# Attention and mixer in one kernel: the last two batches' round trip through DRAM without the turn before it, w2 copied to DRAM in an earlier batch, and another DMA rate in the first part of the plan

## The chip, the cores and the metric

The kernel runs on one core of one Trainium2 chip. The metric is the device time of one execution in microseconds. Before the change, three timed runs gave 572.02, 571.09 and 571.74 us (median 571.74). The profile is one more execution, with a time of 569.56 us of its own.

## The reference, cut to what matters

Four batches of 768 tokens. Attention has 8 heads of width 64; each token sees the tokens less than 16 away, and 24 block keys (the maximum over 32 keys each) with 24 block values (the mean over 32 values each). The mixer follows: a product over tokens, a residual, and a product over channels with a residual.

```python
k_sum = k.reshape(B, H, nb, block, D).max(axis=3)
v_sum = v.reshape(B, H, nb, block, D).mean(axis=3)
scores_l = np.where(mask_l, scale * q @ k.T, -1e9)
scores_s = scale * q @ k_sum.T + np.log(block)
a = softmax(concat(scores_l, scores_s))
x = (a @ concat(v, v_sum))            # (B, 768, 512)
h = np.maximum(x.T @ w_tok1, 0.0) @ w_tok2
u = x + h.T
out = u + np.maximum(u @ w_ch1, 0.0) @ w_ch2
```

All arrays are float32; the weights reach the kernel as pairs of 32-bit words of float64 numbers, so they are decoded on the chip.

## The kernel before, in words

**The plan.** Every piece of work is given to a list with an engine, a cost in microseconds, a rank, the tiles it reads and writes, and for a DMA its size in KB (`Plan.add`, L84). `Plan._order` (L119) then plays the list through once: each engine takes the ready work of lowest rank, and among equals the one listed first. A DMA occupies one shared stream at `RATE` = 250 KB per us and lands `LAND` = 2.2 us later (L72, L151). The order found is written out for each engine and is kept by it; what the chip then does earlier or later than planned does not change it. Tiles of one tag share a ring of buffers in listed order: a tile can be written once the last use of the tile so many places before it is over (`_link`, L107).

**Attention.** A step of `att_step` (L601) is "s" (scores), "e" (the exponentials are turned round so that the keys stand on partitions) or "a" (the weighted sum). `scores` (L401) takes a pair of heads and half of the tokens: 12 products of 64 queries by 120 columns (96 of the window, 24 blocks), then for each of six tiles `lowest` on VectorE (mask and minimum, L441) and `power` on ScalarE (exponential and sum, L451). For batches 0 and 1 the turn is done on TensorE (`turn`, L473). For batches 2 and 3 (`FAR` = 2) it is `turn_blocks` (L504): GpSimd has set the eight unused columns of each 128 to zero (L410), VectorE turns every block of 32 by 32 in place (L512), SyncE writes the tile to DRAM (`away`, L516, 393 KB), and four DMAs of a quarter of the partitions each bring it back with the blocks in their turned places (`fetch`, L525, L531), in runs of 32 numbers (128 bytes). `weighted` (L541) is 24 products on TensorE (L558) for each head and a scaling on VectorE (L571) into x.

**x.** For batches 2 and 3 x is turned on VectorE too (`turn_x`, L634), goes to DRAM in two parts (`xaway`, L645; 512 and 256 tokens for batch 2, 384 and 384 for batch 3), and `fetch_x` (L649) brings each part back in four DMAs in runs of 128 bytes. Batch 2 has it in tiles of tags `e` and `ot`, batch 3 directly in the tiles `u32` of tags `k` and `v`, where it stays to the end. `tok2` (L767) adds it to the product in PSUM on VectorE (L809), splits the sum into two parts (ScalarE L819, VectorE or GpSimd L825), and these feed `ch1`.

**The mixer.** For each half of a batch's tokens and each of 12 slices of the hidden width there is `ch1` (12 matmuls, L853), a relu on ScalarE and the remainder on VectorE (`h`, L865 and L870), and `ch2` (12 matmuls, L896). A half is 512 tokens (the wide half) or 256 (the narrow half). While batch b passes these 24 slots, attention and token mixing of batch b+1 run between the slots, held back so that a scores step does not start before the slot that it was listed in. `ch1` of the next slot is listed before `ch2` of this one. The last batch is done in another form (`last_sums` L1062, `last_mix` L1094): sums of its quarters on VectorE, products with sums of weight quarters, and w2 read back from copies in DRAM that `weight_away` (L1020) makes, 12 copies of 524 KB, in slots 12 to 23 of batch 2.

**The start.** TensorE runs 21 matmuls on zeros, the first keys, queries, the mask and values are loaded, and `w_tick` (L1379) loads and decodes the weights: ScalarE (L1426), VectorE or GpSimd (L1430) and three operations on VectorE (L1435, L1442, L1449). The listed sizes are 737 KB for keys, 393 for queries, 184 for the mask, 295 for values of one head, and 262 for one load of weights.

**Rings that matter here.** Tag `e` has three buffers, for the exponentials, their turned form, the turned x, and the fetched first part of x of batch 2. Scores and weighted sums share the PSUM banks `att`.

Of the kernel before, what the change touches and what calls it, by code (L numbers as in the profile page):

```python
# [69 lines left out]
class Plan:  # L70
    LATE = {"pe": 0.3, "act": 0.15, "dve": 0.15, "pool": 0.2, "sp": 0.0}
    RATE, LAND = 250.0, 2.2  # L72
# [46 lines left out]
    def _order(self):  # L119
# [19 lines left out]
        while events:  # L139
# [5 lines left out]
            for e, queue in queues.items():  # L145
# [45 lines left out]
def tile_attention_mixer(  # L191
# [28 lines left out]
    mask_sb = const.tile([P, 3, NC], F32, name="mask_sb")  # L220
# [51 lines left out]

    def load_q(p):
        b, hp = divmod(p, NP)
        q_t[p] = sbuf([P, S], "q", f"q_{p}", 2)
        return load(q_t[p], lambda t: t, q[b, hp], 393)

    def load_k(p):
        b, hp = divmod(p, NP)
        k_t[p] = sbuf([P, NT, NC], "k", f"k_{p}", 2)  # L280
        return load(k_t[p], lambda t: t, kw[b, hp], 737)
# [23 lines left out]
    def key_blocks(p):  # L305

        if p >= B * NP:
# [6 lines left out]
                in_=kt.t[:, :, 16 : 16 + QT].rearrange("p t (r c) -> p t r c", c=32),  # L314
# [7 lines left out]
                kt.t[:, :, WIN:], ks.t.unsqueeze(1).broadcast_to([P, NT, NB])  # L322
# [78 lines left out]
    def scores(p, g, behind=()):  # L401
# [4 lines left out]
        if p >= FAR * NP:  # L406
# [14 lines left out]
        def products():  # L421
            for i in range(TT // 2):
                for c in range(2):
                    t = 2 * (TT // 2 * g + i) + c
                    for j in range(2):
                        rows = slice(j * D, (j + 1) * D)
                        nc.tensor.matmul(  # L427
                            tiles[j].t[c * QT : (c + 1) * QT, i * NC : (i + 1) * NC],
                            lhsT=qt.t[rows, t * QT : (t + 1) * QT], rhs=kt.t[rows, t, :],
# [4 lines left out]
            "pe", 0.95, products, reads=[(qt, 0), (kt, 0), (kt, 1)],  # L434
            writes=[(t, 0) for t in tiles], rank=R_H, behind=behind,
        )

        def lowest(n, j, i):
# [3 lines left out]
                out=e.t[:, j, i * P : i * P + NC],  # L442
                in0=tiles[j].t[:, i * NC : (i + 1) * NC],
                in1=mask_sb[:, mv, :], op0=ALU.add, op1=ALU.min,
# [3 lines left out]
        def power(n, j, i):  # L448
            T = TT // 2 * g + i
            ei = e.t[:, j, i * P : i * P + NC]  # L450
# [22 lines left out]
    def turn(p, g):  # L473
# [3 lines left out]
        for j in range(2):  # L477
# [7 lines left out]
            eT_t[n, g] = view, [key]  # L485
# [18 lines left out]
    def turn_blocks(p, g):  # L504
# [4 lines left out]
        for j in range(2):  # L509
            eT_t[2 * p + j, g] = (lambda j=j: t_sb.t[:, j]), [(t_sb, r) for r in range(P // 32)]  # L510
        add(
            "dve", 1.05, lambda: nc.vector.transpose(flat(e.t), flat(e.t)),  # L512
            reads=[(e, "ends")], writes=[(e, part) for part in PARTS], rank=R_ATT,
        )
# [4 lines left out]

        fetch(away, t_sb, lambda: flat(t_sb.t), 150)  # L520
# [4 lines left out]
    def fetch(away, slot, view, kb, key=lambda r: r):  # L525


        def part(r):
            rows = slice(32 * r, 32 * (r + 1))
            src = away.t.rearrange("(q p) (t k) -> p t q k", p=32, k=P)  # L530
            nc.sync.dma_start(  # L531
                out=view()[rows].rearrange("p (t q c) -> p t q c", q=P // 32, c=32),
                in_=src[..., rows],
            )

        for r in range(P // 32):
            add(
                "sp", 0.4, lambda r=r: part(r), reads=[(away, 0)], writes=[(slot, key(r))], kb=kb,
            )

    def weighted(p):  # L541
        b, hp = divmod(p, NP)
        if hp % 2 == 0:
            x2_t[b, hp // 2] = sbuf([P, TT, 2, P], "x", f"x_{b}_{hp // 2}", 2)
        x2 = x2_t[b, hp // 2]
        x_t[b, hp] = x2, hp % 2
        for j in range(2):
# [4 lines left out]
            def products(n=n, pt=pt, v=v):  # L552
                pv = pt.t[:, : TT * D].rearrange("p (t d) -> p t d", d=D)
                for T in range(TT):
                    eT = eT_t[n, T // (TT // 2)][0]().rearrange("p (t c) -> p t c", c=P)
                    for c in range(2):
                        cs = slice(c * QT, (c + 1) * QT)
                        nc.tensor.matmul(  # L558
                            pv[cs, T], lhsT=eT[:NC, T % (TT // 2), cs],
# [10 lines left out]
            def scaled(rec=rec, pt=pt, j=j):  # L570
                nc.vector.tensor_tensor(  # L571
# [29 lines left out]
    def att_step(b, s, behind=()):  # L601
# [5 lines left out]
        elif kind == "a":  # L607
            weighted(p)
            if b >= FAR:
                turn_x(b, hp)  # L610
# [17 lines left out]
    def turn_x(b, p):  # L628

        x2, a = x_t[b, p]  # L630
        e = sbuf([P, S], "e", f"xb_{b}_{p}", 3)
        add(
            "dve", 1.05,
            lambda: nc.vector.transpose(  # L634
                e.t.rearrange("p (t c) -> p t c", c=P), x2.t[:, :, a, :]
            ),
# [1030 lines left out]
```

## Time and profile before

| | us |
|---|---|
| median of three runs | 571.74 |
| time of the profiled execution | 569.56 |
| its span in the trace | 567.6 |
| TensorE matmuls busy | 552.1 |
| VectorE busy | 355.6 |
| ScalarE busy | 258.2 |
| GpSimd busy | 258.9 |

The time of the profiled execution is 1.96 us longer than its span: that lies before the first and behind the last instruction. The granted TensorE clock is 1.0 throughout. By stages of the trace: to about 65 us the attention and token mixing of batch 0 with the first weights; 65 to 205 the channel mixing of batch 0 with the attention of batch 1 from about 126 on; 205 to 338 batch 1 with attention of batch 2; 338 to 475 batch 2 with attention of batch 3; 475 to the end the channel mixing of batch 3. The matmuls' ends are modelled, so that a busy share of 100% says only that the next matmul was at hand when the one before it ended. In rows of the timeline, the number in brackets is the idle time in front of an instruction and what ended it.

### The profile page before, as it was taken

To read this page: it belongs to the slowest core of one execution; us is meant where nothing else is said; L and a number is where in the kernel's file an instruction comes from. 1 tells how busy PE (TensorE), PEld (TensorE's weight loads), DVE (VectorE), ACT (ScalarE), POOL (GpSimd) and SP (SyncE) were. 2 spreads that over 40 slices of the span, in tenths; PEclk is the share of its full clock that TensorE was granted. 3 is DMA by queue.
4 is the path that set the end of the run, shared out by engine and by line. 5 is a ranking of instruction groups with operands and counts; after the bars stand their busy time and mean duration, and the time that the engine had idled before them with its cause. 6 is when DMAs were issued, how large, how long until landed. Compare 5 with 4: busy or idle time off the path is not lost.

```text
span 567.6 us, 12757 instructions
## 1 busy us (share of the span) xinstructions
PE 552.1 (97%) x4629; PEld 485.3 (85%) x4629; DVE 355.6 (63%) x982; ACT 258.2 (45%) x789; POOL 258.9 (46%) x325
## 2 busy tenths in 40 slices
PE   7789999999999999999999999999999999999997
PEld 4588888868989988777799997787789999999997
DVE  4698899997474246455563335445352484899984
ACT  4677675437385334232242314242233452567642
POOL 0236586753032510157797511048879711444111
PEclk9999999999999999999999999999999999999999
DMA  8953558653656017758795606677779663643621
GB/s 267 345 169 124 193 191 274 214 179 127 203 157 194 25 39 197 189 182 208 245 261 146 139 13 189 145 189 193 192 182 313 170 263 102 203 131 97 205 92 64
DMA packets 133774, 99.52 MB, mean 175 GB/s; under 512 B 88272, under 2 KB 112464, under 8 KB 133712
## 3 DMA queue, kind: packets, MB, share of 16 engines
q1 hardware_dynamic: 133568, 98.52, 58.2%
q8 instruction: 36, 0.59, 0.4%
q14 instruction: 26, 0.21, 0.1%
q10 hardware_dynamic: 144, 0.20, 0.1%
HBM read 68.60 MB, written 28.31 MB: 171 GB/s over the span
## 4 chain that ended last, share of the span: by engine, by line
PE 76%; DVE 11%; DMA 6%; ACT 3%; issue 2%; POOL 1%; SPq 1%; ACTq 0%; DVEq 0%
PE acc L896 21%; PE hp L853 20%; PE t1q L748 5%; PE up L792 4%; PE av L558 4%; PE pb L1126 3%; PE qb L1126 3%; PE sc L427 3%; DMA w<-in_w_ch 3%; PE qa L1126 2%; PE pc L1126 2%; PE pa L1126 2%; PE qc L1126 2%; DVE wb L1449 2%; ACT e L451 1%
## 5 line engine op out<-in xcount | busy, mean ns | idle before, releaser
L896 PE MATMUL acc<-h,w 128*128 128x512 f32 (+1 forms) x864 | 165.4, 341 | 1.4 <-DVE h L870 1.4
L853 PE MATMUL hp<-u,w 128*128 128x512 f32 (+1 forms) x864 | 163.6, 339 | 0.0
L896 PEld LDWEIGHTS acc<-h,w 128*128 128x128 f32 x864 | 133.4, 189 | 21.9 <-DVE h L870 1.8
L853 PEld LDWEIGHTS hp<-u,w 128*128 128x128 f32 x864 | 133.3, 188 | 20.2 <-issue 1.3
L451 ACT ACTIVATE e<-e,den 128x120 f32<-128x120 f32 x192 | 73.3, 385 | 55.1 <-DVE den L441 39.0
L870 DVE SCALAR_TENSOR_TENSOR h<-hp,h 128x512 fp32r<-128x512 f32 (+1 forms) x72 | 39.7, 552 | 83.8 <-ACT h L865 83.6
L865 ACT ACTIVATE h<-hp 128x512 fp32r<-128x512 f32 (+1 forms) x72 | 35.1, 488 | 114.4 <-PE hp L853 113.3
L973 POOL TENSOR_TENSOR s<-s,w 128x256 f32<-128x256 f32 x84 | 61.7, 741 | 5.0
L441 DVE CUSTOM_DVE_ANT_0 e<-sc,mask_sb 128x120 f32<-128x120 f32 x192 | 41.4, 277 | 13.0 <-PE sc L427 10.8
L1478 POOL TENSOR_TENSOR w<-wb,w 128x256 fp32r<-128x256 f32 x48 | 37.7, 805 | 19.0 <-ACT w L1472 18.8
L935 POOL TENSOR_TENSOR ot<-ot,u 128x512 f32<-128x512 f32 (+1 forms) x24 | 23.8, 1019 | 43.4 <-DVE ot L927 42.6
L792 PE MATMUL up<-wt,t 128*128 128x512 f32 (+2 forms) x192 | 39.0, 343 | 0.0
L451 ACT ACTIVATION_READ_ACCUMULATOR e<-e,den 128x1 f32 x192 | 36.2, 189 | 0.0
L734 POOL TENSOR_TENSOR xs<-x,xs 128x512 fp32r<-128x512 f32 x18 | 23.6, 1310 | 25.5 <-DMA v<-vs 17.9
L410 POOL MEMSET e<- 128x48 f32 x16 | 2.2, 138 | 67.8 <-DMA away<-e 32.7
L792 PEld LDWEIGHTS up<-wt,t 128*128 128x128 f32 x192 | 30.3, 189 | 2.6
L427 PE MATMUL sc<-k,q 64*64 64x120 f32 x768 | 28.1, 271 | 1.9 <-PE et L489 0.7
L427 PEld LDWEIGHTS sc<-k,q 64*64 64x64 f32 x768 | 20.5, 132 | 10.9 <-issue 7.0
L558 PEld LDWEIGHTS av<-v,eT 120*64 120x64 f32 x768 | 24.1, 138 | 6.7 <-issue 4.5
L558 PE MATMUL av<-v,eT 120*64 120x64 f32 x768 | 26.7, 224 | 2.7 <-issue 1.1
L1472 ACT ACTIVATE w<-wb 128x256 fp32r<-128x256 f32 x48 | 18.1, 413 | 23.0 <-DVE wb L1449 22.8
L748 PE MATMUL t1q<-xs,ws 128*128 128x256 f32 x216 | 28.5, 283 | 0.0
(128 smaller groups left out, 862.1 us busy)
## 6 DMA issues: line engine op xcount, KB each, us to landing
w<-in_w_ch SPq DMA_DIRECT2D x48, 256.0 KB
k<-in_kw SPq DMA_DIRECT2D x16, 720.0 KB
v<-in_vw SPq DMA_DIRECT2D x32, 288.0 KB
q<-in_q SPq DMA_DIRECT2D x16, 384.0 KB
away<-e SPq DMA_DIRECT2D x16, 384.0 KB
eT<-away SPq DMA_DIRECT2D x64, 96.0 KB
sums<-s SPq DMA_DIRECT2D x24, 256.0 KB
w2d<-w SPq DMA_DIRECT2D x12, 512.0 KB
```

What stands on the lines that cost most here:

```text
L427: nc.tensor.matmul(tiles[j].t[c * QT : (c + 1) * QT, i * NC : (i + 1) * NC], lhsT=qt.t[rows, t * QT : (t + 1) * QT], rhs=kt.t[rows, t, :], ...
L441: nc.vector.tensor_tensor_reduce(out=e.t[:, j, i * P : i * P + NC], in0=tiles[j].t[:, i * NC : (i + 1) * NC], in1=mask_sb[:, mv, :], op0=A ...
L451: nc.scalar.activation(ei, ei, AF.Exp, bias=den_t[n].t[:, 1, T : T + 1], scale=-1.0, accum_out=den_t[n].t[:, 0, T : T + 1],)
L558: nc.tensor.matmul(pv[cs, T], lhsT=eT[:NC, T % (TT // 2), cs], rhs=v.t[:NC, 2 * T + c], start=True, stop=True,)
L748: nc.tensor.matmul(pt.t[:, 2 * P * k : 2 * P * (k + 1)], lhsT=ws[:, wp, T, ks], rhs=xs[:, xp, T], start=(c == 0 and k == 0 and T == 0 and ...
L792: nc.tensor.matmul(pt.t[:, :nt], lhsT=t1.t[:, part, ks], rhs=wt2[w].t[:, k, h0 : h0 + nt], start=(far and k == 0 and i == 0), stop=(k == D ...
L853: nc.tensor.matmul(pt.t[:, :nt], lhsT=w1_t[f].t[:, w, c], rhs=us[c].t[:, part], start=(i == 0), stop=(i == len(ops) - 1),)
L870: lambda: nc.vector.scalar_tensor_tensor(out=h.t[:, 1], in0=pt.t[:, :nt], scalar=0.0, in1=h.t[:, 0].bitcast(F32), op0=ALU.max, op1=ALU.sub ...
L896: nc.tensor.matmul(slot.t[:, c0 : c0 + nt], lhsT=w2_t[f].t[:, w, o * P : (o + 1) * P], rhs=h.t[:, part], start=(f == 0 and w == 0 and part ...
L973: nc.gpsimd.tensor_tensor(out=out_, in0=left, in1=right, op=op)
L1126: nc.tensor.matmul(bank_.t[:, :HS], lhsT=w(i), rhs=x(j), start=first and n == 0, stop=True, skip_group_check=True,)
L1478: lambda hi=hi, lo=lo, source=source: nc.gpsimd.tensor_tensor(out=lo(), in0=source(), in1=hi().bitcast(F32), op=ALU.subtract),
```

## The change

1. `scores` for batches 2 and 3 multiplies by 128 columns instead of 120: the key tile gets eight more columns behind its last window, set to zero by GpSimd, and the mask tile has 128 columns of which the last eight are -1e30. The eight columns become zero by the exponential itself, and GpSimd's zeroing of the ends (L410) is gone. The exponentials are written in four blocks of 32 columns which stand apart in the tile.
2. `turn_blocks` writes the exponentials to DRAM as they are, `fetch` brings them back into the same tile in runs of 192 numbers (768 bytes), and VectorE then turns them into a second tile.
3. `turn_x` becomes `send_x`: x goes to DRAM unturned, straight from its tile, and `fetch_x` brings it back in runs of 256, 384 or 512 bytes. VectorE turns it afterwards: in place for batch 2, from a tile of tag `e` into `u32` for batch 3. The fetches of batch 3 are listed in slot 17, in the order in which the token mixing uses them, where before they were listed in slots 16 and 17.
4. The copies of w2 to DRAM are listed in slots 12 to 23 of batch 0 instead of batch 2.
5. The plan counts DMAs at 360 KB per us instead of 250 for those that it starts before 25 us of its own time.

```diff
-    RATE, LAND = 250.0, 2.2
+    RATE, FIRST, LAND = 250.0, 360.0, 2.2
-                    dma = max(dma, now) + w.kb / self.RATE
+                    dma = max(dma, now) + w.kb / (self.RATE if now > 25 else self.FIRST)
...
-            add(
-                "pool", 0.2,
-                lambda: nc.gpsimd.memset(
-                    e.t.rearrange("p j (t c) -> p (j t) c", c=P)[:, :, NC:], 0.0
-                ),
-                writes=[(e, "ends")], rank=R_LATER,
-            )
+        far = p >= FAR * NP
+        wide = P if far else NC
...
-                            tiles[j].t[c * QT : (c + 1) * QT, i * NC : (i + 1) * NC],
-                            lhsT=qt.t[rows, t * QT : (t + 1) * QT], rhs=kt.t[rows, t, :],
+                            tiles[j].t[c * QT : (c + 1) * QT, i * wide : (i + 1) * wide],
+                            lhsT=qt.t[rows, t * QT : (t + 1) * QT],
+                            rhs=kt.t[rows, t * NC : t * NC + wide],
...
-        add(
-            "dve", 1.05, lambda: nc.vector.transpose(flat(e.t), flat(e.t)),
-            reads=[(e, "ends")], writes=[(e, part) for part in PARTS], rank=R_ATT,
-        )
         add(
             "sp", 0.4, lambda: nc.sync.dma_start(out=away.t, in_=flat(e.t)),
             reads=[(e, part) for part in PARTS], writes=[(away, 0)], kb=393,
         )
-        fetch(away, t_sb, lambda: flat(t_sb.t), 150)
+        fetch(away, e, lambda: flat(e.t), 110)
+        add(
+            "dve", 1.05,
+            lambda: nc.vector.transpose(
+                flat(t_sb.t).rearrange("p (x a c) -> p a x c", a=P // 32, c=32),
+                flat(e.t).rearrange("p (a x c) -> p a x c", a=P // 32, c=32),
+            ),
+            reads=[(e, r) for r in range(P // 32)], writes=[(t_sb, 0)], rank=R_ATT,
+        )
...
-            src = away.t.rearrange("(q p) (t k) -> p t q k", p=32, k=P)
+            src = away.t.rearrange("(a p) (b c) -> p b a c", p=32, b=P // 32)
             nc.sync.dma_start(
-                out=view()[rows].rearrange("p (t q c) -> p t q c", q=P // 32, c=32),
-                in_=src[..., rows],
+                out=view()[rows].rearrange("p (a c) -> p a c", a=P // 32), in_=src[:, r]
             )
...
-        add(
-            "dve", 1.05,
-            lambda: nc.vector.transpose(
-                e.t.rearrange("p (t c) -> p t c", c=P), x2.t[:, :, a, :]
-            ),
-            reads=x_keys(b, p), writes=[(e, 0)], rank=R_ATT,
-        )
...
+        tag, bufs = (("e", 3), ("ot", 2))[half and not whole]
+        slot = sbuf([P, nt], tag, f"xT_{b}_{half}_{p}", bufs)
+        parts = [(slot, r) for r in range(P // 32)]
+        fetch(xa_t.pop((b, half, p)), slot, lambda: slot.t, nt // 6)
+        if whole:
+            to, j = u32[half, p // 2], p % 2
+            xT_t[b, half, p] = lambda: tokens(to.t[:, j]), [(to, j)]
+            add(
+                "dve", 0.07 + nt / 780,
+                lambda: nc.vector.transpose(tokens(to.t[:, j]), blocked(slot.t)),
+                reads=parts, writes=[(to, j)], rank=R_EVAC,
+            )
+        else:
+            xT_t[b, half, p] = lambda: blocked(slot.t), parts
+            add(
+                "dve", 0.07 + nt / 780, lambda: nc.vector.transpose(slot.t, slot.t),
+                writes=parts, rank=R_EVAC,
+            )
...
-            if b + 1 == B - 1 and slot in (16, 17):
-                for h in range(2):
-                    for p in (2 * slot - 32, 2 * slot - 31):
-                        fetch_x(b + 1, h, p)
+            if b + 1 == B - 1 and slot == 17:
+                for _, h, p in t2s:
+                    fetch_x(b + 1, h, p)
...
-            if b == B - 2 and slot >= NF:
+            if b == 0 and slot >= NF:
                 weight_away(slot - NF)
```

More of the change, by code (lines that the diff above doesn't have):

```diff
@@ L219, in tile_attention_mixer @@
     make_identity(nc, identf)
-    mask_sb = const.tile([P, 3, NC], F32, name="mask_sb")
+    mask_sb = const.tile([P, 3, P], F32, name="mask_sb")
+    nc.gpsimd.memset(mask_sb[:, :, NC:], -1.0e30)
     means = const.tile([WIN, 2 * NB - 2], F32, name="means")
@@ L271, in load, with windows @@
         )
+    def windows(t):
+        return t[:, : NT * NC].rearrange("p (t c) -> p t c", c=NC)
     def load_q(p):
@@ L279, in load_k @@
         b, hp = divmod(p, NP)
-        k_t[p] = sbuf([P, NT, NC], "k", f"k_{p}", 2)
-        return load(k_t[p], lambda t: t, kw[b, hp], 737)
+        slot = k_t[p] = sbuf([P, NT * NC + P - NC], "k", f"k_{p}", 2)
+        if b >= FAR:
+            add(
+                "pool", 0.1, lambda: nc.gpsimd.memset(slot.t[:, NT * NC :], 0.0),
+                writes=[(slot, "pad")], rank=R_ATT,
+            )
+        return load(slot, windows, kw[b, hp], 737)
     def load_v(n):
@@ L441, in lowest @@
             nc.vector.tensor_tensor_reduce(
-                out=e.t[:, j, i * P : i * P + NC],
-                in0=tiles[j].t[:, i * NC : (i + 1) * NC],
-                in1=mask_sb[:, mv, :], op0=ALU.add, op1=ALU.min,
+                out=block(j, i), in0=shaped(tiles[j].t[:, i * wide : (i + 1) * wide]),
+                in1=shaped(mask_sb[:, mv, :wide]), op0=ALU.add, op1=ALU.min,
                 scale=-1.0 / 8.0, scalar=3.0e38, accum_out=den_t[n].t[:, 1, T : T + 1],
@@ L537, in fetch @@
             add(
-                "sp", 0.4, lambda r=r: part(r), reads=[(away, 0)], writes=[(slot, key(r))], kb=kb,
+                "sp", 0.4, lambda r=r: part(r), reads=[(away, 0)], writes=[(slot, r)], kb=kb,
             )
@@ L647, in turn_x @@
             )
     def fetch_x(b, half, p):
-        if b == B - 1:
-            g, j = divmod(p, 2)
-            if not j:
-                u32[half, g] = sbuf([P, 2, HS], "kv"[g], f"u32_{half}_{g}", 2)
-            slot = u32[half, g]
-            xT_t[b, half, p] = lambda: slot.t[:, j], [(slot, (j, r)) for r in range(P // 32)]
-            fetch(
-                xa_t.pop((b, half, p)), slot, lambda: slot.t[:, j], HT[b][half] // 5,
-                lambda r: (j, r),
-            )
-            return
@@ L661, in fetch_x @@
-        tag, bufs = (("e", 3), ("ot", 2))[half]
-        slot = sbuf([P, HT[b][half]], tag, f"xT_{b}_{half}_{p}", bufs)
-        xT_t[b, half, p] = lambda: slot.t, [(slot, r) for r in range(P // 32)]
-        fetch(xa_t.pop((b, half, p)), slot, lambda: slot.t, HT[b][half] // 5)
+        nt, whole = HT[b][half], b == B - 1
+        if whole and (half, p // 2) not in u32:
+            u32[half, p // 2] = sbuf([P, 2, HS], "kv"[p // 2], f"u32_{half}_{p // 2}", 2)
+        tag, bufs = (("e", 3), ("ot", 2))[half and not whole]
@@ L809, in tok2 @@
                 lambda: nc.vector.tensor_tensor(
-                    out=xT(), in0=pt.t[:, :nt], in1=xT(), op=ALU.add
+                    out=xT(), in0=tokens(pt.t[:, :nt]), in1=xT(), op=ALU.add
                 ),
-                reads=[(pt, 0)], writes=parts + ([(u32[half, p // 2], p % 2)] if whole else []),
-                rank=R_EVAC,
+                reads=[(pt, 0)], writes=parts, rank=R_EVAC,
             )
@@ L824, in tok2 @@
                 eng, took,
-                lambda: between(eng, u.t[:, 1], xT(), u.t[:, 0].bitcast(F32), ALU.subtract),
+                lambda: (nc.vector, nc.gpsimd)[half].tensor_tensor(
+                    out=tokens(u.t[:, 1]), in0=xT(),
+                    in1=tokens(u.t[:, 0].bitcast(F32)), op=ALU.subtract,
+                ),
                 reads=[*parts, (u, 0)], writes=[(u, 1)], rank=R_EVAC,
```

83 lines of the change are left out of this document (60 added, 23 removed).

## The prediction

> **What bounds the kernel now.** I read the page first, then busy time by stage, then the chain of waits, then the timelines of the places that the change touches. In the page:
>
> ```profile
> span 567.6 us, 12757 instructions
> PE 552.1 (97%) x4629; PEld 485.3 (85%) x4629; DVE 355.6 (63%) x982; ACT 258.2 (45%) x789; POOL 258.9 (46%) x325
> DMA packets 133774, 99.52 MB, mean 175 GB/s; under 512 B 88272, under 2 KB 112464, under 8 KB 133712
> ```
>
> TensorE idles for 567.6 - 552.1 = 15.5 us in all, and nothing here makes its matmuls fewer. By stages (TensorE, weight loads, VectorE, ScalarE, GpSimd busy; clock, DMA share, GB/s):
>
> ```profile
> 0.00:20.00 20.00, 15.61 (x239) 9.94 (x241) 7.54 (x48) 10.67 (x45) 3.96 (x11) 1.00 0.92 295
> ...
> 80.00:100.00 20.00, 20.00 (x87) 16.14 (x86) 19.45 (x36) 12.58 (x29) 14.81 (x23) 1.00 0.81 252
> ...
> 140.00:160.00 20.00, 19.64 (x281) 18.00 (x279) 11.63 (x46) 9.41 (x38) 3.30 (x3) 1.00 0.55 179
> 160.00:180.00 20.00, 19.57 (x268) 18.73 (x269) 12.42 (x60) 13.36 (x52) 5.36 (x6) 1.00 0.65 202
> 180.00:200.00 20.00, 20.00 (x157) 19.29 (x156) 6.12 (x15) 8.05 (x17) 10.50 (x9) 1.00 0.17 49
> ...
> 380.00:400.00 20.00, 19.39 (x144) 15.34 (x143) 9.60 (x36) 6.56 (x27) 17.66 (x26) 1.00 0.73 185
> ```
>
> More than a quarter of it lies in the first 20 us (4.39), 0.79 in 140 to 180, and 0.61 at 380 to 400; of the stages from 205 to 475, in which batches 2 and 3 pass their attention, that last window is the only one short of 20.00. There TensorE is the bound, VectorE has 9.60 of 20 and the DMA engines are not full (0.73). So the part of the change that is longest in code can give back 0.61 us; the start, which only the plan's new rate touches, has more.
>
> **The change part by part.** *Runs through DRAM.* Runs of 128 bytes: 32 x 24 in each of 64 fetches of exponentials, 49,152, and 3,072 for each of 8 tiles of x, 24,576; together 73,728 of the 88,272 short packets. After it 64 x 32 x 4 = 8,192 runs of 768 bytes for the exponentials, 8,192 of 256 to 512 for x, and 8,192 more where x is written out. Who waits for them today:
>
> ```profile
> 373.43 6.17 DMA away<-e
> ...
> 379.61 0.58 SPq L531
> ...
> 381.64 3.91 DMA eT<-away
> 385.69 1.27 PE av L558 x36
> 341.54 0.78 PE sc L427 x24
> 456.79 4.17 PE up L792 x24
> 475.02 1.07 PE pa L1126 x6
> 148.16 6.51 DMA k<-in_kw
> ```
>
> ```profile
> 385.69 1.27 PE L558 MATMUL av<-v,eT 120*64 120x64 f32 x36 [0.61 <-DMA eT<-away]
> ```
>
> The fetch landed 3.91 us after the last of its four issues, and the later matmuls of one weighted sum waited 0.61 us for it, the only such wait among TensorE's. I take it away: **-0.6** (0 if it stays). [...]
>
> *Wider scores.* A pair of heads takes 0.78 us for half of the tokens. If columns set its pace, 128 instead of 120 add 0.78 x 8/120 = 0.052, 16 times: 0.83; if weight loads do, nothing. TensorE is the bound there, so **+0.8**, bounds 0 and 0.83. The same eight columns on ScalarE and VectorE (192 tiles of 385 and 277 ns, half of them far) add at most 96 x 26 and 96 x 18 ns, hidden under matmuls while VectorE stands at half. GpSimd loses 16 small fills and gains 8, at most 17.66 of 20 busy there.
>
> *The turns' new place.*
>
> ```profile
> L512 DVE STREAM_TRANSPOSE e<-e 128x768 f32<-128x768 f32 x16 | 15.6, 972 | 10.9 <-ACT e L451 9.5 <-POOL s L973 1.2
> L634 DVE STREAM_TRANSPOSE xb<-x 128x768 f32<-128x768 f32 x8 | 7.8, 978 | 0.3
> L451 ACT ACTIVATE e<-e,den 128x120 f32<-128x120 f32 x192 | 73.3, 385 | 55.1 <-DVE den L441 39.0 <-DMA v<-in_vw 16.0
> L441 DVE CUSTOM_DVE_ANT_0 e<-sc,mask_sb 128x120 f32<-128x120 f32 x192 | 41.4, 277 | 13.0 <-PE sc L427 10.8 <-DMA away<-e 2.1
> ```
>
> The blocks turned stay the same, 15.6 + 7.8 us; x's 8 turns become 16 shorter ones. But now each waits for a fetch, with VectorE's later work behind it in its order: the next `lowest`, and the remainder `h` for which `ch2` waits. A late fetch costs TensorE only what exceeds the cover: the next slot's 12 matmuls run while `h` is made.
>
> ```profile
> 378.82 2.96 PE L853 MATMUL hp<-u,w 128*128 128x512 f32 x12
> 381.62 2.96 PE L896 MATMUL acc<-h,w 128*128 128x512 f32 x12
> 382.45 0.69 DVE L870 SCALAR_TENSOR_TENSOR h<-hp,h 128x512 fp32r<-128x512 f32 x1 [1.42 <-ACT h L865]
> 318.82 0.69 DVE L809 TENSOR_TENSOR xT<-up,xT 128x512 f32<-128x512 f32 x1 [5.83 <-DMA xT<-xaway]
> 321.41 0.41 DVE L870 SCALAR_TENSOR_TENSOR h<-hp,h 128x256 fp32r<-128x256 f32 x1
> 425.44 0.39 ACT L865 ACTIVATE h<-hp 128x256 fp32r<-128x256 f32 x1 [0.67 <-PE hp L853]
> ```
>
> In the wide half slots of matmuls start 381.62 - 378.82 = 2.80 apart, and relu (estimated at 0.5 from its 0.39 in the narrow half) and remainder (0.69) take 1.2: cover 1.6. In the narrow half 1.4, half of that, less 0.39 and 0.41: 0.6. VectorE already stood 5.83 us for a fetch at 318.82, and the windows there show TensorE without a pause, because the list had put other matmuls ahead. So I take **0**; bounds 0 and +3.2 (rival B). The held buffers: a tile of exponentials is now busy until its turn, some fetch (4 to 6 us) longer, and the next scores wait for it; pairs of heads follow each other every 25 us (the weighted sums at 385.69 and, two pairs later, at 436.66 below), and the chain scores, exponentials 4, away 6, fetch 6, turn 1, sum 2 is about 20, so it fits without spare.
>
> *x of batch 3 at the end of batch 2.* Today its fetches run from 394 on; then they share `e`'s three buffers and cannot start before the last weighted sum:
>
> ```profile
> 436.66 1.62 PE L558 MATMUL av<-v,eT 120*64 120x64 f32 x48
> 394.20 2.96 SPq L531 DMA_DIRECT2D u<-xaway  x4
> 446.71 4.89 SPq L531 DMA_DIRECT2D u<-xaway  x7
> 462.11 0.55 DVE L809 TENSOR_TENSOR u<-up,u 128x384 f32<-128x384 f32 x1
> 468.00 1.02 DVE L975 SCALAR_TENSOR_TENSOR t<-t,t 128x384 fp32r<-128x384 f32 x2
> ```
>
> 32 issues at about 0.65 us (4.89 / 7 is 0.70, with other work of the queue between) are 21 us: from 437 to 458, landed and turned by 461. The last addition is at 462.11 now, so nothing is late by itself. Eight turns of about 0.49 us (384 of 768) delay VectorE's sums from 469 to perhaps 473; the last batch starts at 475.02, behind 14 us of channel matmuls. **0**; without that cover each us late is one lost.
>
> *w2's copies.*
>
> ```profile
> 461.35 3.08 SPq L1023 DMA_DIRECT2D w2d<-w  x4
> 460.00:470.00 10.00, 10.00 (x85) 10.00 (x84) 9.14 (x21) 5.68 (x14) 1.02 (x1) 1.00 0.61 237
> ```
>
> 524 KB at 237 GB/s is 2.2 us each, or 1.35 at a full share (237 / 0.61). Where they leave (424 to 464) TensorE has no idle time to win. In batch 0's second half, 134 to 205, one comes every 6 us: the share rises by 0.23 to 0.37, from 0.55 and 0.65 to nearly full, on the queue that brings batch 1's keys. DMA waits of 3.05 (block values), 6.51 (the quoted keys) and 1.90 us are on the chain there, 11.46 in all, and TensorE lost 0.36 + 0.43 us: 7%. Each longer by 2.2 gives 6.6 x 7% = **+0.5**; bounds 0 and 6.6.
>
> *The rate of the first 25 us.* By the listed sizes 5,016 KB go up to and with the first load of weights: planned to land at 5,016 / 250 + 2.2 = 22.3 us, now at 5,016 / 360 + 2.2 = 16.1. At the measured 295 GB/s it is 17.0. What the list does with it today:
>
> ```profile
> 19.87 0.56 DVE L571 TENSOR_TENSOR x<-av,rec 128x384 f32<-128x384 f32 x1 [4.70 <-PE av L558]
> 23.66 0.43 DVE L1430 TENSOR_SCALAR wt<-wt 128x512 f32<-128x512 f32 x1 [0.48 <-ACT wt L1426]
> ...
> 25.31 0.69 DVE L1449 SCALAR_TENSOR_TENSOR wt<-w,wt 128x512 int32<-128x512 int32 x1
> 30.74 0.40 ACT L451 ACTIVATE e<-e,den 128x120 f32<-128x120 f32 x1 [3.33 <-DVE den L441]
> 117.94 2.60 PE L896 MATMUL acc<-h,w 128*128 128x512 f32 x10 [1.40 <-DVE h L870]
> ```
>
> VectorE stands 4.70 us up to 19.87, begins decoding at 23.66, and the decodes then hold up ScalarE's exponentials for 3.33 us. One decode, four operations, is 25.31 + 0.69 - 23.66 = 2.3 us and would fit between 17.0 and 19.87. From 80 to 100 VectorE is busy 19.45 of 20 us and TensorE waits for it at 117.94, so time won there reaches the matmuls. I take one decode, less a little for the order around it, **-2.2**; bounds -4.7 (the whole gap) and +0.9 (planned at 16.1, there at 17.0, and VectorE standing).
>
> Sum: -0.6 + 0.8 + 0 + 0 + 0.5 - 2.2 = **-1.5**. The profiled execution is 569.56 (span 567.6 and 1.96 around it) and would be 568.1. The median of the runs is 2.2 above it; I carry the difference over: 571.74 - 1.5 = **570.2**.
>
> **The rivals.** *A, nothing in the start:* the wait at 19.87 is for a matmul, not for weights, and the list may fill the gap with something that was no bound. Then -0.6 + 0.8 + 0.5 = +0.7: 572.4. For it: only ScalarE's 3.33 us show that decoding came at a bad time. *B, slower: VectorE's list stands for fetches.* Place: the turns in narrow halves, 4 of exponentials and 12 of x; it decides once a fetch is later than its turn's place by more than 0.6 us. Four issues and landing took 5.94 us (379.61 to 385.55, chain of waits) where the plan now gives 4 x 110 / 250 + 2.2 = 3.96. If half of the 16 are late by 1.0, (1.0 - 0.6) x 8 = 3.2: 573.4. Against it: 5.83 us of the same wait cost nothing at 318.82. [...] *C, slower: copies in front of keys*, none covered: 570.2 + 6.6 - 0.5 = 576.3; against it, the plan counts the copies and puts matmuls ahead. *D, the whole gap of the start won:* 570.2 - 2.5 = 567.7.
>
> **How the numbers follow.** The forecast gets 0.42, A 0.18, B 0.21, C 0.07, D 0.12. About 0.2% (1.1 us) is what a measurement of this kernel can tell from no change. The forecast's own range is 569.0 to 571.5, with 0.7 of it below 570.6: 0.30 faster; with D 0.42. Same: 0.12 of the forecast, 0.14 of A and 0.02 of B, 0.28. Slower: the rest of A and B, and C, 0.30. The range 567.2 to 574.6 leaves out C and the tails of B and D.
>
> **What would show it.** Right: VectorE's gap before the first x gone and the first decode near 17 us; the dense channel matmuls some 2 us earlier; scores of batches 2 and 3 at 0.83; short packets about 31,000 or fewer; no TensorE idle time on a fetch between 205 and 475. Wrong: TensorE waiting for `h` with VectorE standing before a turn (B), key loads over 8 us between 140 and 180 (C), the first decode still after 22 us (A), or idle time before 475 because x of batch 3 came late.

## The result, and the profile after

The changed kernel took 574.1 us (median of nine runs, 572.96 to 575.23) where the kernel before took 571.09 beside it: a ratio of 1.0054, 95% interval 1.0034 to 1.0073. In a later group of runs (e9 below) it took 572.96 against 571.61, 1.0026 (1.0002 to 1.0050). So it is slower by 1.4 to 3 us, where 1.5 us faster was forecast. The profiled execution took 574.1 us. Three lines of its page:

```profile
span 572.3 us, 12735 instructions
...
PE 556.1 (97%) x4629; PEld 489.4 (86%) x4629; DVE 361.1 (63%) x990; ACT 260.1 (45%) x789; POOL 257.5 (45%) x318
...
DMA packets 82830, 99.52 MB, mean 174 GB/s; under 512 B 27216, under 2 KB 62032, under 8 KB 82768
```

The short packets went from 88,272 to 27,216, as the change says. TensorE's idle time is 572.3 - 556.1 = 16.2 us, hardly more than the 15.5 before; its matmuls' busy time grew by 4.0 us, so lost time can hide in matmuls that take longer. Where it lies, by the start of four matmul groups (first channel matmul of batch 0, first wide slot of batches 1 and 2, first product of the last batch), each read from TensorE's timeline:

| us | batch 0 | batch 1 | batch 2 | last batch | lengths between |
|---|---|---|---|---|---|
| before | 65.53 | 205.10 | 338.57 | 474.86 | 139.57, 133.47, 136.29 |
| changed | 70.20 | 207.87 | 342.00 | 479.59 | 137.67, 134.13, 137.59 |

Four differences add up to the 4.7 us between the last two starts: the first channel matmul comes 4.67 later, batch 0's stage is 1.90 shorter, batch 1's 0.66 longer and batch 2's 1.30 longer. The two profiled executions are 4.5 us apart where the medians are 3.0 apart: the one of before ran at the full clock throughout (a mean of 1.000), which 8 of 133 executions do (last section).

**The start.** Four-microsecond windows of the changed kernel (the busy time of the five engines, then granted clock, DMA share, GB/s), and its waits of TensorE and VectorE:

```profile
8.00:12.00 4.00, 1.72 (x51) 1.36 (x50) 2.97 (x21) 1.78 (x9) 0.00 (x0) 1.00 1.04 305
12.00:16.00 4.00, 3.17 (x49) 2.96 (x49) 0.63 (x8) 2.05 (x12) 0.00 (x0) 0.56 1.02 303
16.00:20.00 4.00, 4.00 (x72) 3.36 (x72) 2.41 (x15) 3.08 (x13) 1.59 (x2) 0.59 1.04 388
```

```profile
PE vm L348 <- DMA v<-in_vw: 5.2, 4, 2.3
PE t1p L739 <- DVE wt L1501: 2.7, 1, 2.7
```

```profile
DVE ks L321 <- DMA k<-in_kw: 10.1, 3, 4.2
DVE x L599 <- PE av L577: 1.4, 1, 1.4
```

The same windows of the kernel before:

```profile
8.00:12.00 4.00, 2.45 (x50) 1.60 (x42) 3.41 (x25) 3.12 (x17) 0.00 (x0) 1.00 1.05 278
12.00:16.00 4.00, 3.48 (x78) 2.93 (x78) 2.09 (x20) 3.98 (x20) 0.00 (x0) 1.00 1.03 281
16.00:20.00 4.00, 2.87 (x86) 2.63 (x88) 0.13 (x1) 2.29 (x10) 3.19 (x4) 1.00 1.03 382
```

VectorE's gap of 4.70 us ahead of the first x has shrunk to 1.4, as forecast, but the decoding did not move into it: the first decode is at 24.23, later than the 23.66 of before. VectorE stands for keys instead:

```profile
16.81 0.95 DVE L321 TENSOR_REDUCE ks<-k 128x24 f32<-128x768 f32 x1 [4.18 <-DMA k<-in_kw]
...
24.23 0.43 DVE L1482 TENSOR_SCALAR wt<-wt 128x512 f32<-128x512 f32 x1 [0.41 <-ACT wt L1478]
```

These waits are 10.1 us in three places, where the kernel before had one:

```profile
DVE ks L312 <- DMA k<-in_kw: 3.3, 1, 3.3
```

So 6.8 us more of VectorE's time go to waiting for keys, and 5.2 us of TensorE's to waiting for values, in a list that expects data at 360 KB per us while the DMA engines move 305 and 303 GB/s from 8 to 16 us; another 2.7 us of TensorE's go to waiting for decoded weights. And the granted clock, 1.00 before, is 0.56 and 0.59 from 12 to 20 us: from 12 to 16 us 49 small matmuls hold TensorE for 3.17 us, where 78 took 3.48.

**The end of batch 2.** TensorE, VectorE and SyncE's queue in the changed kernel:

```profile
456.14 0.62 PE L842 MATMUL up<-wt,t 128*128 128x384 f32 x2
457.05 0.97 PE L842 MATMUL up<-wt,t 128*128 128x384 f32 x4 [0.29 <-DVE t L725]
457.86 1.59 PE L948 MATMUL acc<-h,w 128*128 128x256 f32 x12
459.29 3.29 PE L842 MATMUL up<-wt,t 128*128 128x384 f32 x18
463.01 1.31 PE L842 MATMUL up<-wt,t 128*128 128x384 f32 x6 [0.44 <-DVE u L859]
```

```profile
455.32 0.58 DVE L687 STREAM_TRANSPOSE u<-xT 128x384 f32<-128x384 f32 x1 [0.33 <-DMA xT<-xaway]
...
458.45 0.58 DVE L687 STREAM_TRANSPOSE u<-xT 128x384 f32<-128x384 f32 x1 [1.45 <-DMA xT<-xaway]
...
462.42 0.54 DVE L859 TENSOR_TENSOR u<-up,u 128x384 f32<-128x384 f32 x1
```

```profile
434.39 6.21 SPq L550 DMA_DIRECT2D xT<-xaway  x6
440.77 1.21 SPq L666 DMA_DIRECT2D xaway<-x  x2
442.02 12.22 SPq L550 DMA_DIRECT2D xT<-xaway  x23
454.34 0.38 SPq L1066 DMA_DIRECT2D sums<-s  x1
454.77 1.39 SPq L550 DMA_DIRECT2D xT<-xaway  x3
```

The 32 issues for x of batch 3 fill the queue from 434 to 456. VectorE's turns stand for them, its splits and additions stand behind the turns, and the token products `up` wait 0.29 and 0.44 us for those and start piecewise.

**What stayed quiet.** Scores, two groups in a row, before and after; the turns; and the windows in which w2 is now copied:

```profile
345.24 0.85 PE L427 MATMUL sc<-k,q 64*64 64x120 f32 x24
346.02 3.06 PE L896 MATMUL acc<-h,w 128*128 128x512 f32 x12
```

```profile
344.90 0.89 PE L429 MATMUL sc<-k,q 64*64 64x128 f32 x24
345.72 3.07 PE L905 MATMUL hp<-u,w 128*128 128x512 f32 x12
```

```profile
L534 DVE STREAM_TRANSPOSE eT<-e 128x768 f32<-128x768 f32 x16 | 15.6, 972 | 6.3 <-DMA e<-away 6.3
L687 DVE STREAM_TRANSPOSE u<-xT 128x384 f32<-128x384 f32 x8 | 4.6, 575 | 6.0 <-DMA xT<-xaway 6.0
```

```profile
140.00:160.00 20.00, 20.00 (x242) 18.53 (x241) 12.21 (x53) 9.75 (x38) 5.11 (x4) 1.00 0.76 251
160.00:180.00 20.00, 20.00 (x291) 18.96 (x290) 11.52 (x59) 14.37 (x59) 5.28 (x6) 1.00 0.83 266
...
380.00:400.00 20.00, 19.99 (x173) 15.86 (x172) 9.08 (x27) 5.87 (x22) 15.85 (x22) 1.00 0.59 180
```

A group of scores takes 345.72 - 344.90 = 0.82 us where it took 0.78. VectorE stands 6.3 us in front of the turns of exponentials and TensorE loses nothing by it. From 140 to 180 and from 380 to 400 TensorE is full.

### The profile page after: what moved, and what is told of

Read it like the earlier page. It is cut to its first block, busy times and chain, and to the rows that moved or that the text cites. A ratio compares the mean times of both kernels' runs of the same rounds, so it can differ in the third digit from the quotient of the medians.

```text
span 572.3 us, 12735 instructions
## 1 busy us (share of the span) xinstructions
PE 556.1 (97%) x4629; PEld 489.4 (86%) x4629; DVE 361.1 (63%) x990; ACT 260.1 (45%) x789; POOL 257.5 (45%) x318
## 2 busy tenths in 40 slices
DMA packets 82830, 99.52 MB, mean 174 GB/s; under 512 B 27216, under 2 KB 62032, under 8 KB 82768
## 4 chain that ended last, share of the span: by engine, by line
PE 79%; DVE 9%; DMA 5%; issue 2%; ACT 2%; SPq 2%; POOL 1%; DVEq 0%; ACTq 0%
PE acc L948 23%; PE hp L905 22%; PE av L577 4%; PE sc L429 4%; PE up L842 4%; PE t1q L798 4%; PE qb L1178 3%; PE pb L1178 3%; PE qa L1178 2%; PE pc L1178 2%; PE pa L1178 2%; PE qc L1178 2%; DVE wb L1494 2%; DVE wb L1501 2%; DMA v<-in_vw 2%
## 5 line engine op out<-in xcount | busy, mean ns | idle before, releaser
L463 ACT ACTIVATE e<-e,den 128x120 f32<-128x120 f32 (+1 forms) x192 | 74.0, 387 | 39.4 <-DVE den L454 39.1
L454 DVE CUSTOM_DVE_ANT_0 e<-sc,mask_sb 128x120 f32<-128x120 f32 (+1 forms) x192 | 42.6, 280 | 8.1 <-PE sc L429 7.7
L429 PE MATMUL sc<-k,q 64*64 64x120 f32 (+1 forms) x768 | 28.9, 282 | 0.8 <-DVE den L454 0.8
L321 DVE TENSOR_REDUCE ks<-k 128x24 f32<-128x768 f32 x16 | 15.2, 947 | 22.8 <-DMA k<-in_kw 22.8
```

What stands on the lines that cost most here:

```text
L429: nc.tensor.matmul(tiles[j].t[c * QT : (c + 1) * QT, i * wide : (i + 1) * wide], lhsT=qt.t[rows, t * QT : (t + 1) * QT], rhs=kt.t[rows, t ...
L454: nc.vector.tensor_tensor_reduce(out=block(j, i), in0=shaped(tiles[j].t[:, i * wide : (i + 1) * wide]), in1=shaped(mask_sb[:, mv, :wide]), ...
L463: nc.scalar.activation(ei, ei, AF.Exp, bias=den_t[n].t[:, 1, T : T + 1], scale=-1.0, accum_out=den_t[n].t[:, 0, T : T + 1],)
```

## The experiments

All ratios are to the kernel before, run on the same chip, with 95% intervals. The runs came in four groups, each with its own runs of the kernel before: e1 to e4 and e13 to e15 on one chip, e5 to e8 and e9 to e12 on another. A difference of two kernels is taken within a group unless the text says otherwise.

### e1 to e3: the parts alone

e1, only the rate, in the kernel before:

```diff
-    RATE, LAND = 250.0, 2.2
+    RATE, FIRST, LAND = 250.0, 360.0, 2.2
...
-                    dma = max(dma, now) + w.kb / self.RATE
+                    dma = max(dma, now) + w.kb / (self.RATE if now > 25 else self.FIRST)
```

> The kernel before with one change: the plan counts DMAs that it starts before 25 us at 360 KB per us instead of 250. Theory (the loss is made in the start, by a list that expects keys and values earlier than they land): the first matmul of the first channel product, at 65.53 us before and 70.20 after, is at 69.5 to 70.5 here, and the time is 2.5 to 4.5 us above the kernel before. Rivals (the turns that wait for fetches, or the copies of w2, make the loss): within 1 us of the kernel before.

e2, the changed kernel with the old rate:

```diff
-    RATE, FIRST, LAND = 250.0, 360.0, 2.2
+    RATE, FIRST, LAND = 250.0, 250.0, 2.2
```

> The changed kernel with the old rate of 250 KB per us in the whole plan. Theory: the first channel product is back at 65.5 us; what is left is wider scores 16 x 0.045 = +0.7, weighted sums split in two +0.3, waits of 0.7 before the last batch, less the 0.6 us wait on a fetch that is gone: 1.1 us above the kernel before (0 to 2). Rivals: as slow as the changed kernel, 2.5 to 4 us above the kernel before.

e3, only w2's copies, in the kernel before:

```diff
-            if b == B - 2 and slot >= NF:
+            if b == 0 and slot >= NF:
```

> The kernel before with the copies of w2 listed in batch 0 instead of batch 2. Theory: within 1 us of the kernel before, as the changed kernel shows no new wait of TensorE between 140 and 205 us. Rival (copies in front of key loads): 2 to 6 us slower, with idle time of TensorE between 140 and 180 us.

e1: 572.51 us, 1.0022 (1.0000 to 1.0045). e2: 572.86, 1.0024 (0.9999 to 1.0049). e3: 571.21, 0.9983 (0.9962 to 1.0003). The rate alone costs about 1.3 us (0 to 2.6), where 2.5 to 4.5 were expected, and the rest without it about as much; w2 sooner costs nothing and may win a little. The first channel matmul misses both expectations: 66.81 in e1, not near 70, and 68.32 in e2, not back at 65.5. In e2's profile the stage of batch 2 is 137.9 us long, in e1's 136.1: that loss belongs to the new path of x and exponentials.

### e4 and e5: is the start's loss the granted clock?

e3 has the first 25 us of the kernel before in the same order, and yet its profile shows another clock (busy time of TensorE, clock, DMA share, GB/s):

```profile
12.00:16.00 4.00, 3.44 (x56) 0.75 1.02 323
16.00:20.00 4.00, 4.00 (x58) 0.50 1.04 383
20.00:24.00 4.00, 4.00 (x103) 0.90 0.33 112
```

(0.25 + 0.50 + 0.10) x 4 = 3.4 us of clock lost, with the first channel matmul at 67.74 in place of 65.53. e4 and e5 put matmuls on zeros into TensorE's pauses; nothing reads them.

e4, the changed kernel:

```diff
+            if p == 0 and g == 1:
+                for _ in range(14):
+                    nc.tensor.matmul(pw.t, lhsT=warm.t[:, :P], rhs=warm.t, start=True, stop=True)
...
```

> The changed kernel, the same list on every engine, but with 14 more matmuls on zeros (some 3 us) on TensorE directly behind the first two scores, where it stood idle 2.28 and 0.82 us for values. It separates the waiting from the clock: the granted clock of the changed kernel is 0.56 from 12 to 16 us and 0.59 from 16 to 20. If the lower clock behind the idle time is a cause of its own, the clock is 1.0 in those windows and the first channel product comes 1 to 3 us sooner (67 to 69 us); if only the late loads count, it stays at 70.2 within 0.4 and the time does not move.

e5, the kernel before: three such matmuls behind the first scores, two behind each of the first two turns.

```diff
+            for _ in range(3 if fill else 0):
+                nc.tensor.matmul(pw.t, lhsT=warm.t[:, :P], rhs=warm.t, start=True, stop=True)
...
+                for _ in range(2 if fill else 0):
+                    nc.tensor.matmul(pw.t, lhsT=warm.t[:, :P], rhs=warm.t, start=True, stop=True)
...
```

> The kernel before, with seven matmuls on zeros added to TensorE's list in its pauses of the start (three behind the first scores, two behind each of the first two turns); the result is untouched. Clock theory (idle time of TensorE in the start lowers the granted clock, and that is what makes one execution of the same list longer than another): the granted clock of 8 to 24 us stays near 1.0, the first channel matmul starts near 65.5 (65.53 in the profile of before, 67.74 with the same list at a lowered clock), the median falls by 1 to 2 us (ratio 0.9965 to 0.998) and its spread gets narrower. Rival (the pauses matter only as waits): the seven matmuls, 7 x 0.23 = 1.6 us in pauses of 0.7, 0.4 and 0.5 us, change nothing or cost some tenths: ratio 1.000 to 1.001.

e4: 571.83 us, 0.9994 (0.9978 to 1.0011); its clock is 1.00 from 8 to 24 us (and lowered later, from 24 to 36) and its first channel matmul at 67.45, as the clock theory had it. e5: 571.37, 1.0017 (0.9994 to 1.0040): no gain, though its mean granted clock rose from the 0.9936 of the kernel before beside it to 0.9962. The theory that filled pauses shorten the kernel fell here; where the time went that the clock should have given is not shown.

### e6: x of batch 3 written in quarters

In the changed kernel with the old rate, each part of x of batch 3 goes out in four DMAs and comes back in one, in rows of 1,536 bytes: 8 issues behind the last weighted sum in place of 32. TensorE's order is that of e2.

```diff
...
-        fetch(xa_t.pop((b, half, p)), slot, lambda: slot.t, nt // 6)
+        away = xa_t.pop((b, half, p))
+        if whole:
+            add(
+                "sp", 0.4, lambda: nc.sync.dma_start(out=slot.t, in_=away.t),
+                reads=[(away, r) for r in range(P // 32)], writes=parts, kb=nt // 2,
+            )
+        else:
+            fetch(away, slot, lambda: slot.t, nt // 6)
```

> The changed kernel with the rate of before, in which x of batch 3 is written to DRAM in four pieces for each part and comes back in one DMA with rows of 1,536 bytes in place of four; TensorE's order is the same as in e2. Theory (the end of batch 2 loses its 1.3 to 1.6 us because 32 issues for x of batch 3, 17 us of the queue, can begin only behind the last weighted sum): the 8 issues are through some 10 us sooner, TensorE's waits of 0.3 + 0.3 us before the token products go, and these run in one piece (9.8 us busy back to 9.2); the stage of batch 2 is 136.0 to 136.5 long in place of 137.9, and the median falls by 1.3 to 1.6 us against e2 (ratio to before about 0.9998). Rival (VectorE's eight turns and its order, not the queue, hold the additions back): the stage stays at 137.5 or more and the ratio at 1.002.

572.3 us, 1.0007 (0.9976 to 1.0037). The stage is 478.35 - 341.76 = 136.59 long where e2's was 137.94: 1.35 us less, by the same order of matmuls, and TensorE waits for nothing there. The time alone would not have settled it.

### e7 and e8: a rate near the measured one; w2 with filler

e7 is the kernel before with another rate; the second line of e1's edit belongs to it too.

```diff
-    RATE, LAND = 250.0, 2.2
+    RATE, FIRST, LAND = 250.0, 300.0, 2.2
...
```

> The kernel before with a rate of 300 KB per us for the DMAs of the first 25 us, near the 295 GB/s measured in the first 20 us, in place of 360. If 360 does harm because it is above the real rate and puts work at times at which its data isn't there, 300 has waits of TensorE for values in the start of under 1 us together (4.1 us with 360) and a ratio to before of 0.996 to 1.000. If any other order of the start loses against the one of before, it is 1.001 to 1.003, as with 360 (1.0022).

e8 is e3 with the filler of e5.

> The kernel before with the copies of w2 in batch 0 (e3, ratio 0.9983) and the seven matmuls on zeros of e5 in the pauses of the start. If the two add up: 0.9983 times the ratio of e5, by the clock theory 0.995 to 0.9965, the fastest of all so far. If the filler does nothing, 0.998 to 0.999.

e7: 570.98 us, 0.9997 (0.9973 to 1.0020). e8: 570.63, 0.9985 (0.9959 to 1.0011), as e3 without the filler. Another order of the start does not have to lose, but the reason given for e7 missed: TensorE still waits 2.2 us for values in its start, where under 1 was expected.

### e9 to e12: the changed kernel again, and the filler once more

e9 is the changed kernel, e10 is e4 with e6's edit, e11 is e1 with e4's 14 matmuls, e12 is e11 with e3's edit.

> The changed kernel once more, beside the next three on one chip, as their yardstick: 3.0 us above the kernel before (ratio 1.0054, 1.0034 to 1.0073) if what was measured first holds on another chip; granted clock of 0.5 to 0.8 somewhere between 12 and 36 us if the pause of TensorE for the values (3.1 us at 9.5 to 12.9) always lowers it.

> The changed kernel with the 14 matmuls on zeros of e4 (they fill TensorE's pause for the first values; the result is untouched) and with x of batch 3 written in four pieces and read in one (e6). If the two losses, the start's and the one at the end of batch 2, are separate: e4 against the changed kernel is worth 2.3 us and e6 against e2 shortened the stage by 1.35, together 3.6 us under e9 and 0.3 to 0.9 us under the kernel before (ratio 0.9985 to 0.9995). If they hide each other: 1.000 or more.

> The kernel before with the rate of 360 (e1, ratio 1.0022) and the 14 matmuls on zeros behind the first two scores. Theory (the rate's list loses by TensorE standing still for the values, which lowers its clock afterwards; the list itself isn't worse): 2 to 2.5 us under e1, ratio 0.998 to 0.999, the clock at 1.0 up to 24 us. Rival (the list is worse because of its waits for data, and filling them gains nothing; what e4 won came from the chip that it ran on): 1.001 to 1.003.

> e11 with the copies of w2 in batch 0 as well (e3, ratio 0.9983). If what each brings adds up, 0.9965 to 0.9975, faster than the kernel before beyond the interval; if the copies bring nothing by themselves, as e11.

e9: 572.96 us, 1.0026, less than half of the 3.0 us of the first measurement; its clock is lowered in the same windows. e10: 571.25, 1.0001 (0.9981 to 1.0021), 1.7 below e9 where 3.6 were expected, and e6's edit explains 1.35 of it. e11: 572.81, 1.0029 (0.9999 to 1.0059), no better than e1, though its clock was 1.00 up to 24 us. e12: 570.48, 0.9991 (0.9970 to 1.0013), better than e11 and short of the sum. The filler earns nothing on the rate's list either; most of what e4 seemed to win against the 574.1 of the first measurement did not hold within one group.

### e13 to e15: the two losses mended

e13 is e3 with the rate of 300, e14 the changed kernel with 300, e15 is e14 with e6's edit.

> The kernel before with a rate of 300 for the first 25 us and the copies of w2 in batch 0. e3 (w2 alone) gave 0.9983 and e7 (300 alone) 0.9997. If the two add up: 0.998, about 570.5 us where the kernel before has 571.5; if w2's copies were chance: 1.000.

> The changed kernel with a rate of 300 in place of 360, all else as changed. Over 104 executions of the kernel before, the time rises by 0.32 us for each 0.001 that the mean granted clock falls (569.3 at 1.0); with 360 the mean clock is 0.9906 in the changed kernel and 0.9894 in e1, with 300 it was 0.9922 in e7, where the time was 0.3 under the kernel before. If the start's loss comes from the rate being above the real one: 1 to 1.5 us under the changed kernel, ratio 1.001 to 1.003, the stage of batch 2 still 137.6 to 137.9 long. Rival (any reordering of the start costs as much): as the changed kernel, 1.0026 to 1.0054.

> e14 with x of batch 3 written in four pieces and read in one, as in e6: the whole change with its two losses mended. The stage of batch 2 comes to 136.3 to 136.6 and the time to 1.2 to 1.4 us under e14: ratio 0.9985 to 1.0005. What is left against the kernel before is the wider scores, 16 x 0.045 = 0.7 us. Rival (the end of batch 2 was not the loss): no difference from e14.

e13: 569.02 us, 0.9962 (0.9943 to 0.9980), faster than both kernels. e14: 570.97, 0.9990 (0.9972 to 1.0008). e15: 569.61, 0.9971 (0.9954 to 0.9987). All three came out faster than expected. VectorE's waits in e13, with its first x and its first decoding operation; TensorE's waits for values in e13, and for values and decoded weights in e14; and the end of batch 2 in e15, with the queue:

```profile
DVE ks L312 <- DMA k<-in_kw: 3.1, 1, 3.1
...
DVE x L571 <- PE av L558: 0.5, 1, 0.5
```

```profile
18.06 0.91 DVE L312 TENSOR_REDUCE ks<-k 128x24 f32<-128x768 f32 x1
...
19.78 1.26 DVE L571 TENSOR_TENSOR x<-av,rec 128x384 f32<-128x384 f32 x2 [0.46 <-PE av L558]
...
21.48 0.43 DVE L1430 TENSOR_SCALAR wt<-wt 128x512 f32<-128x512 f32 x1
```

```profile
PE vm L339 <- DMA v<-in_vw: 4.2, 3, 3.2
```

```profile
PE vm L348 <- DMA v<-in_vw: 2.6, 3, 1.0
PE t1p L739 <- DVE wt L1501: 1.2, 1, 1.2
```

```profile
453.46 4.33 PE L866 MATMUL up<-wt,t 128*128 128x384 f32 x24
...
473.05 1.23 PE L1202 MATMUL pa<-u,w 128*128 128x384 f32 x6
```

```profile
433.10 2.42 SPq L701 DMA_DIRECT2D xT<-xaway  x3
435.67 3.67 SPq L667 DMA_DIRECT2D xaway<-x  x8
439.44 5.21 SPq L701 DMA_DIRECT2D xT<-xaway  x5
```

At 300 the gap in front of x shrinks too (0.5 us in e13, 1.4 in e14, no more than 0.8 in e15) and no wait for keys stands in its place (3.0 to 3.1 us in all three, 3.3 before). What moves ahead of x is not the decoding but the minima and key sums of the next heads, and decoding, behind x as before, begins at 21.48 in e13 where it began at 23.66. TensorE still waits for values. In e15 the fetches are issued by 445 and the products run 24 in a row. In all three the clock is lowered in the start as well (e13: 0.60 from 12 to 16 us), so the lower clock does not make a list lose by itself.

The profiles of all runs, read up to batch 0's last slot, show two effects apart. "Clock" is the time lost to a lowered clock in the first 64 us; "idle" is TensorE's idle time before the first channel matmul and within batch 0's stage (from there to the first wide slot of batch 1):

| | rate | w2 copied in batch | clock, us | first channel matmul | idle | stage of batch 0 | idle |
|---|---|---|---|---|---|---|---|
| before | 250 | 2 | 0 | 65.53 | 9.0 | 139.57 | 2.2 |
| e3 | 250 | 0 | 3.4 | 67.74 | 7.5 | 140.08 | 2.7 |
| e7 | 300 | 2 | 5.1 | 66.40 | 6.6 | 140.33 | 3.0 |
| e1 | 360 | 2 | 3.4 | 66.81 | 8.7 | 139.80 | 2.7 |
| e13 | 300 | 0 | 3.4 | 65.58 | 7.4 | 137.89 | 1.0 |
| e14 | 300 | 0 | 5.1 | 66.88 | 7.1 | 137.74 | 0.9 |
| changed | 360 | 0 | 5.1 | 70.20 | 10.9 | 137.67 | 0.8 |

First, the rate: e14 and the changed kernel lose the same clock, and the changed kernel comes 3.3 us later (e9, again with 5.1, 3.6 later), with 3.8 us more idle time; so in these executions it is the waits and not the clock that separate 360 from 300. In the kernel before, TensorE's idle time there is 2.1 us more at 360 (e1) than at 300 (e7). Secondly, batch 0's stage is 137.6 to 138.3 us long in all eight profiles with a higher rate and w2's copies in batch 0, and 139.4 to 140.8 in the nine with one of them or neither. The two together win some 2 us there that neither wins alone.

The parts add up within the last group: e13 is 2.50 us below the kernel before; the wider scores add 0.7, which gives -1.8, and e15 measured -1.91; x of batch 3 late adds e14 - e15 = 1.36, which gives -0.55. Each of these times is known to about 1 us, so that the agreement to 0.1 is in part luck. From there to the changed kernel there is only the rate, 300 to 360: 1.9 us by e9's distance from its own kernel before (1.35 + 0.55), 3.6 by the first measurement's (3.01 + 0.55), each across groups. Against the old rate of 250 (e2, 1.0024) 360 costs the changed kernel only 0.1 to 1.7 us: in the profiles, both with 5.1 us of clock lost, it reaches the first channel matmul 1.9 us later than e2 (70.20, 68.32) and has a stage of batch 0 that is 1.7 us shorter (137.67, 139.40).

## Why the prediction was wrong

**Right.** The fetch stall (-0.6): the window 380 to 400 is full (19.99 of 20). That the fetch would land sooner was the author's assumption, which no run of before shows; in the changed kernel, where a turn waits for four issues in a row, issues and landing take 3.9 to 4.8 us (311.20 to 315.17, 386.41 to 391.23, 429.36 to 433.22), where the prediction read 5.94. The wider scores (+0.8): 0.82 - 0.78 is 0.04 to 0.05 a group, 0.7 in 16. The turns' new place (0): 6.3 us of VectorE standing before the turns of exponentials reached no matmul, for the profile shows no wait of TensorE from 205 to 440. Short packets: 27,216 against "31,000 or fewer".

**The rate of the first 25 us (-2.2) failed,** in two steps. The first is the step that put a decode into VectorE's gap ("would fit between 17.0 and 19.87"). Nowhere in the changed kernel, e1, e13 and e14 does the decoding begin before the first x: it is at 24.23, 21.62, 21.48 and 23.44. Its first operation on VectorE also stands behind one on ScalarE, which begins at 22.97 before and at 23.53 in the changed kernel and which the prediction left out. The list may fill the gap with other work, as rival A said. The second is the step that took 360 for nearly harmless: the bound "+0.9 (planned at 16.1, there at 17.0, and VectorE standing)" priced one late load, the weights. But a list made for 360 also expects keys and values, which come before the weights, too soon, and an order that is kept stands for them: 6.8 us more of VectorE's time for keys than before, and on TensorE 5.2 us for values and 2.7 for decoded weights, where e14, at 300, has 2.6 and 1.2. The prediction had the number that says so, 295 GB/s beside 360, and used it for one load only. Measured: about +1.3 alone (e1, 0 to 2.6) where -2.2 stood; e14 against the changed kernel puts 360 at 1.9 to 3.6 us above 300.

That e13 wins 2.5 us, near the 2.2 of the forecast, does not bear out the sum. The rate of 300 alone (e7) won nothing that could be measured, and a good part of e13's gain is the stage of batch 0 (1.7 us shorter in its profile), which needs w2's copies as well, a term that stood at +0.5. The wait for `h` at 117.94, through which won time was to reach the matmuls, is gone in the changed kernel; in e1 and e7 the stage has no less idle time than before.

**x of batch 3 (0) failed:** 1.36 us. The step was "the last addition is at 462.11 now, so nothing is late by itself", with 14 us of channel matmuls as the cover before the last batch. The last batch was indeed not what waited. TensorE's own order has the token products of batch 3 between those channel matmuls, each needs a split and a free bank from VectorE, and VectorE stood at a turn in front of both. That is the mechanism of rival B, in the place where B counted 12 turns of x, but it ended in `up` and not in `h`, and cost 1.36 rather than 3.2. The 21 us of issues came out (434 to 456), partly by luck: an issue was priced at 0.65, but the 23 in one row took 0.53 each and the first six 6.21 together.

**w2's copies (+0.5)** cost nothing: e3 is 1.0 us under the kernel before (interval -2.2 to +0.2), and beside e7 (0.9997) e13 (0.9962) is even faster with them. The waits of 0.36 and 0.43 us between 140 and 180 are gone in the changed order. Rival C's loss does not show: from 120 to 200 VectorE waits 2.0 us for keys in the changed kernel where it waited 5.1 before, and TensorE for nothing from 140 to 205.

**The carried difference did not hold either.** The forecast took the profiled execution, 569.56, as 2.2 us below the median for no reason of its own. It had one: its granted clock was 1.0 throughout the start, and 125 of 133 executions have a mean below 1.000 (see the last section). Of 21 executions of the changed kernel none is above a mean of 0.994, and those of e9 have 0.9906 on average against 0.9931 in the 133 of before; by the slope in the last section that would be some 0.8 us of its loss, an estimate.

What stays open: why a higher rate and the earlier copies shorten batch 0's stage only together, and what the lowered clock costs by itself; the fillers raised the clock and gave no time. The 0.66 us that batch 1's stage lost is 8 x 0.045 = 0.36 of scores; the rest was not traced.

## What to carry to other kernels

In the changed kernel the one of three rates that lies near the measured one was the best (ratios 0.9990 at 300, 1.0024 at 250, 1.0026 and 1.0054 at 360): the list made for 360 stood at loads that it expected too soon, VectorE 10.1 us for keys and TensorE 5.2 us for values. Before a gap is credited to a change, ask which work the planner will put into it; here it was other work than the decoding. Parts that win nothing alone may win together, so that tests one by one do not give the sum. When a wait moves to another engine, look not only at the end that it threatens but at what stands in each engine's order between there and here. And when a profile is compared with a median, compare the granted clock first.

## What the runs showed of the hardware

The granted clock in the start differs between executions of the same order, and about half of the variance of this kernel's times goes with it. Five values of the mean granted clock, some 0.003 apart, hold 94 of the 133 timed executions of the kernel before in the four groups:

```
mean clock   executions   mean us
1.000             8        568.98
0.997            21        570.64
0.994            31        571.32
0.991            16        571.85
0.988            18        573.15
```

The other 39 scatter about the same line (at 0.996, 12 executions have a mean of 569.82; at 0.987, 8 have 572.28). Over all 133 the time rises by 0.31 us for each 0.001 that the mean clock falls, with a correlation of -0.72 (squared, 0.52). The profiles show where: in 12 to 40 us, in stretches that cost 0, 3.4 or 5.1 us of clock in the first 64 us in every profile kept (3.4 in e3 by its rows above; 5.1 in the changed kernel, (0.44 + 0.41) x 4 from its rows and 0.43 x 4 from 32 to 40), multiples of 1.7. Apart from the start, the profiles of e6 and e8 show one such step more, 1.7 us between 116 and 128 (clock 0.69 and 0.88 in two windows of 4 us, and 0.85 and 0.72). What lowers the clock, and why it differs from execution to execution, is not shown. The pauses of TensorE directly ahead of e3's lowered clock are 0.69, 0.43 and 0.54 us between 10.2 and 13.3, with two short groups of transposes, 0.70 us each, between them. The kernel before has the same stretch from 9.1 to 12.2 (0.68, 0.43 and 0.54) and no lowered clock behind it (1.00 from 12 to 24), so that these pauses by themselves do not lower it.

The issues of the 64 fetches of exponentials on the queue, before with 768 runs each and changed with 128 (shortest, median and longest in ns, then first and last start):

```profile
L531 SPq DMA_DIRECT2D eT<-away x64: 557/657/2141, 219.8 to 431.0; - x64
```

```profile
L550 SPq DMA_DIRECT2D e<-away x64: 318/430/1214, 217.5 to 430.7; - x64
```

A sixth of the runs shortens the median issue from 0.66 to 0.43 us only, far less than in proportion, so that the number of issues sets much of the length of the queue. That agrees with e6's edit, which moves issues from the read to the write and won 1.36 us (e15 against e14) with the same bytes.
